# RetNet attention into a SwiGLU block in fp32: the gate/value products of the 1024-token tiles by Strassen's scheme applied twice, in place of a 26-product scheme

## The chip, the cores and the metric

One core of a Trainium2 chip runs the kernel. The metric is device microseconds of one execution; the runs of the kernel before took 1037.82, 1038.73 and 1038.70 us (median 1038.7). Engines are named as in the profile: PE (TensorE's matmuls), PEld (its weight loads), DVE (VectorE), ACT (ScalarE), POOL (GpSimd), SP (SyncE, which here issues DMAs).

## The reference

All arrays are fp32. Eight batches of eight heads, 576 positions, head size 64; the attention's heads are laid side by side to give 4608 tokens of 512 features, which go through a SwiGLU block with 1536 hidden features.

```python
scores = scale * np.matmul(q, k.transpose(0, 1, 3, 2))
Dmat = np.where(rel >= 0, gamma[:, None, None] ** rel[None, :, :], 0.0)
attn = np.matmul(scores * Dmat[None], v)
x = attn.transpose(0, 2, 1, 3).reshape(B * S, H * D)      # 4608 x 512
g, val = x @ w_gate, x @ w_val                            # 512 x 1536 each
return (g * (1.0 / (1.0 + np.exp(-g))) * val) @ w_out     # 1536 x 512
```

## The kernel before

The tokens are cut into a first tile of 512 (number 0, done with plain matmuls) and four tiles of 1024 (numbers 1 to 4). The attention of one batch and one pair of heads is a "tick"; it makes `x` for its tokens, and ticks for the next tile are spread through the current one, so tile 4 has none. Small pieces of a tick (copies, masks, decays, transposes) wait in the list `pieces` and are run by `part_on` between matmul steps; the last piece of a tick issues the loads of a later one (`next_load`) on SP.

Each 1024-token tile has an "up" stage (gate and value, `up_step`) and a "down" stage (`down_step`, output product). In the up stage, the 1536 hidden features are three "quarters" of 512 (`NQ` = 3, index `qd`; the name comes from the arena's layout). For a quarter, a 512x512 weight matrix (gate and value side by side) times 512x1024 of `x` is done by a scheme of 26 products. Its table `UP` gives for each of the 26 steps the bank, the sums of `x` and of weights to be made, the operands, and what to do with the result. A step is four matmuls of 128x128 by 256 columns (gate and value, two contraction halves) into one PSUM bank of 128x512. TensorE runs an fp32 matmul as two records, so a step shows as eight. Four banks (A, B, C, E) are used in rotation (`rested`).

What comes off a bank is copied by ACT, or added to an earlier partial result by DVE; `reads` also sends additions between partial results in SBUF to POOL (DVE in tile 1, partly). When a block of the hidden matrix is done, ACT applies Silu to its gate half into `io`, and DVE or POOL multiplies with the value half into `hid`.

Tile 1 differs: its weight sums are made then (`w_sums` on POOL, negations on ACT), and every weight operand is written to DRAM (`up_ops`, a DMA issued by ACT at line 1128). In tiles 2 to 4 the operands come back through a ring of eight SBUF slots (`fetch`, on SP, line 1022). The down stage's operands (`dn_ops`) come through the same ring; it overlaps the place of the weights, so that the first eight fetches of tile 1's down operands are made when weights are dead: at steps 21, 22 and 25 of the last quarter.

The order on every engine is the order in which the program is written (`manual_schedule`); `merge` interleaves ticks and steps evenly. Every queue runs in order, so a waiting instruction holds all behind it. SBUF is full: places are reused by hand (`part` for partial results, `xsum` for sums of `x`).

Of the kernel before, what the change touches and what calls it, by code (L numbers as in the profile page):

```python
# [22 lines left out]
def tables(gamma, scale, L):  # L23
# [27 lines left out]
UP = [  # L51
    "0= | 8: sub 8 2 6, sub 9 0 8, sub 10 4 9 | 8: neg 8 6, sub 9 2 6, sub 10 3 7, add 11 1 10 | copy 0, copy 1",
    "1= | 10: sub 11 3 8, sub 12 7 11 | 3: nad 12 3 6 | copy 2, copy 3",
    "2= | 0:  | 9:  | copy 4, copy 5",
    "3= | 12:  | 11: sub 8 11 6 | copy 6",
    "0+ | 9:  | 12: add 9 2 3 | sub 2 b 2, sub 4 4 2, out 4 4",
    "1= | 4: sub 13 0 2 | 10: nad 11 11 0 | add 2 b 2, neg 12 2",
    "3+ | 11: add 14 4 12 | 8:  | add 1 b 1",
    "0+ | 13: sub 15 14 0 | 9: add 12 4 5, add 10 2 12, nad 8 7 10 | sub 5 5 b, out 6 5",
    "1+ | 14: sub 16 0 1, add 17 5 16 | 11:  | add 6 b 6",  # L60
    "3= | 15: sub 18 4 6, sub 19 5 18 | 0: add 6 6 7 | add 7 b 6, neg 0 7",
    "2+ | 17:  | 8: sub 9 3 0 | copy 4",
    "0= | 19: add 20 7 10 | 5: add 11 0 2 | copy 5",
    "1= | 6:  | 6: add 7 7 5 | sub 0 b 0, out 14 0",
    "3+ | 20: sub 21 4 17 | 9: add 8 5 6 | sub 3 b 3",
    "2= | 3: sub 22 16 6 | 11: add 0 0 1 | add 7 b 3, out 7 7",
    "0+ | 21: add 18 18 7 | 7: nad 9 1 3 | add 2 b 2, sub 4 4 2, add 5 5 4",
    "1+ | 22:  | 8: sub 11 1 10 | add 2 b 2, neg 13 2",
    "3= | 18: sub 23 1 3, sub 24 5 23 | 0: nad 6 6 12 | add 6 b 6",
    "0= | 7:  | 9: add 2 2 4 | add 1 b 1, add 3 b 3, neg 15 1, neg 3 3, add 6 6 3, neg 2 6",  # L70
    "2+ | 24: sub 1 1 5 | 11: sub 12 0 12 | add 3 b 3",
    "1+ | 16:  | 6:  | sub 4 b 4",
    "3= | 1: sub 2 16 2 | 2: sub 1 5 1 | sub 5 b 5, add 0 b 4, out 8 5, out 9 0",
    "2+ | 23: sub 25 7 24 | 12: nad 3 3 10 | add 7 b 4, out 1 7",
    "1+ | 2:  | 4:  | neg 10 b",
    "3+ | 25:  | 1:  | sub 3 b 3, out 11 3",
    "0= | 5:  | 3:  | add 4 b 4, neg 5 4",
]
# [77 lines left out]
def kernel(  # L156
# [32 lines left out]
    nc = tc.nc  # L189
# [60 lines left out]
    at = [4096 + 512 * i for i in range(4)] + [x0_at + 512 * i for i in range(4)]  # L250
    at += [dn_at + 4096 + 512 * i for i in range(6)] + [part_at + 512 * i for i in range(4)]
    xsum = [rest[:, a : a + 512] for a in at]
    part = [rest[:, dn_at + 512 * i : dn_at + 512 * (i + 1)] for i in range(8)] + xsum[14:18]
# [642 lines left out]

    up, down = lines(UP), lines(DOWN)
    N = len(up)
# [13 lines left out]
    up_ops = [[dr.tile([P, 512], F32, name=f"up{qd}_{i}") for i in range(N)] for qd in range(NQ)]  # L912
# [85 lines left out]
    def up_view(qd):  # L998
        return lambda s: (w_up[:, qd, :, s // 2, s % 2, :] if s < 8
                          else extra[:, s - 8].rearrange("p (g x) -> p g x", g=2))  # L1000

    def x_view(n):
        return lambda s: (xs[n][:, 2 * (s // 4) : 2 * (s // 4) + 2, (s % 4) * TB : (s % 4 + 1) * TB] if s < 8
                          else xsum[s - 8].rearrange("p (c x) -> p c x", c=2))
# [6 lines left out]
    fetches = [("dn", 1, i) for i in range(N)]  # L1011
    for n in range(2, NTILE):
        fetches += [("up", qd, i) for qd in range(NQ) for i in range(N)] + [("dn", n, i) for i in range(N)]
    fetched = [0]
    turn = [5, 4, 1, 6, 7, 2, 0, 3]

    def fetch():
        m = fetched[0]
        if m < len(fetches):
            what, a, i = fetches[m]  # L1020
            src = up_ops[a][i] if what == "up" else dn_ops[i]
            nc.sync.dma_start(out=ring[:, turn[m % 8], 0 : src.shape[-1]], in_=src)
            fetched[0] += 1
# [22 lines left out]
    products = []  # L1046

    def reads(ops, bank, busy, result, spread=False):

        at = lambda a: bank if a == "b" else part[int(a)]  # L1050
        old = len(products)
        for op in ops:
            if op[0] in ("copy", "add", "sub"):
                while any(a == op[1] for a, _ in products):
                    products.pop(0)[1]()
                    old -= 1
            if op[0] == "copy":
                nc.scalar.copy(out=at(op[1]), in_=bank)
            elif op[0] in ("add", "sub"):
                eng = nc.vector if "b" in op or (busy and not spread) else nc.gpsimd  # L1060
                eng.tensor_tensor(out=at(op[1]), in0=at(op[2]), in1=at(op[3]),  # L1061
                                  op=ALU.add if op[0] == "add" else ALU.subtract)
            else:
                product = result(int(op[1]), at(op[2]), op[0] == "neg", op[2] == "b" or busy)
                if product and op[2] == "b":
                    product()
                elif product:
                    products.append((op[2], product))
        for _ in range(old):
            products.pop(0)[1]()  # L1070


    x_ops = [op for line in up for op in line[3]]
    X_FIRST = 8

    def x_sums(n, lo, hi, vector):
        for op in x_ops[lo:hi]:
            add(nc.vector if vector or op[0] == "nad" else nc.gpsimd, op, x_view(n))

    def negated(qd, i):  # L1080

        view = up_view(qd)
        for op in up[i][5]:
            if op[0] == "nad":
                nc.scalar.mul(out=view(int(op[1])), in_=view(int(op[3] if op[3] == op[1] else op[2])), mul=-1.0)

    def w_sums(qd, i):
        view = up_view(qd)
        for op in up[i][5]:
            if op[0] == "nad":  # L1090

                dst, a, b = [view(int(s)) for s in op[1:]]
                if op[3] == op[1]:
                    a, b = b, a
                nc.gpsimd.tensor_tensor(out=dst, in0=dst, in1=b, op=ALU.subtract)
            else:
                add(nc.gpsimd, op, view)

    def first_sums(qd, lo, hi):

        engines = [nc.scalar, nc.gpsimd, nc.vector, nc.gpsimd]
        for op, eng in list(zip(up[0][5], engines, strict=True))[lo:hi]:
            if op[0] == "neg":
                nc.scalar.mul(out=up_view(qd)(int(op[1])), in_=up_view(qd)(int(op[2])), mul=-1.0)
            else:
                add(eng, op, up_view(qd))

    def up_step(n, qd, i):
        label, opens, xslot, _, wslot, _, ops = up[i]
        busy = n == 1  # L1110
        if qd == 0:
            done = lambda i: X_FIRST + (min(3 * i, 2 * i + 2, i + 6) if busy else i)
            x_sums(n, done(i), done(i + 1), busy)
        if busy:
            if i > 1:
                w_sums(qd, i)
            w = up_view(qd)(wslot)
        else:
            w = operand()[:, 0:512].rearrange("p (g x) -> p g x", g=2)
        rhs = x_view(n)(xslot)  # L1120
        b = bank(label, i == 0)
        for gv in range(2):
            for c in range(2):
                m = nc.tensor.matmul(b[:, gv * TB : (gv + 1) * TB], w[:, gv, ts(c, P)], rhs[:, c, :],  # L1124
                                     start=(opens and gv == 0 and c == 0), stop=(c == 1), skip_group_check=True)
        stepped.append(m)
        if busy:
            nc.scalar.dma_start(out=up_ops[qd][i].rearrange("p (g x) -> p g x", g=2), in_=w)
            if i in (20, 23) and qd + 1 < NQ:
                first_sums(qd + 1, *((0, 2) if i == 20 else (2, 4)))  # L1130
            if i == 24 and qd + 1 < NQ:
                negated(qd + 1, 1)
                w_sums(qd + 1, 1)
            if 0 < i < N - 1:
                negated(qd, i + 1)
            if qd + 1 == NQ:
                for _ in range({21: 3, 22: 2, N - 1: 3}.get(i, 0)):
                    fetch()
        else:
            fetch()  # L1140

        def result(o, src, negative, vector):
            s = io[:, (silus[0] % 4) * TB : (silus[0] % 4 + 1) * TB]
            silus[0] += 1
            nc.scalar.activation(out=s, in_=src[:, 0:TB], func=AF.Silu, scale=-1.0 if negative else 1.0)  # L1145
            dst = hid[:, qd, o // 4, o % 4]
            if negative:
# [8 lines left out]
        if qd + 1 == NQ and i + 1 == N:  # L1156
            while products:
                products.pop(0)[1]()
# [187 lines left out]
```

## Time and profile before

| | us |
|---|---|
| median of three runs (lowest, highest) | 1038.7 (1037.82, 1038.73) |
| profiled execution, first to last instruction | 1037.2 |
| up stage of tile 1, 2, 3, 4 | 146.7, 145.2, 139.6, 134.6 |
| down stage of tile 1, 2, 3, 4 | 79.7, 77.1, 69.3, 71.0 |
| before tile 1 | 174.0 |

The profile comes from one execution. For it only the span is given: 1037.2 us, 1.5 below the median of the timed runs, and all working below is made against that span. Busy times are sums over the span or over a stated stretch; a chain of waits follows the last instruction back through what released it; a group of instructions shows count, busy time, mean duration, and idle time before with what ended it. PE records are pipelined, and their durations overlap; the time of a matmul is read from the spacing of steps. The granted clock was 0.998 over the span.

### The profile page before, as it was taken

How to read it: one execution, taken by the hardware profiler on the slowest of the kernel's cores; microseconds unless marked ns; L12 is line 12 of the kernel's file. 1: busy time of each engine (PE TensorE's matmuls, PEld its weight loads, DVE VectorE, ACT ScalarE, POOL GpSimd, SP SyncE). 2: the span in 40 equal slices, each digit the busy share in tenths (PEclk: the TensorE clock that was granted, in tenths of full speed). 3: DMA queues.
4: the chain of work that ended last, by engine and by line, in shares of the span. 5: the costliest groups of instructions: out<-in, count | busy, mean ns of one | idle time of the engine just before them, and what ended most of it. 6: DMA issues, size and time to landing. Idle time of an engine off the chain costs nothing.

```text
span 1037.2 us, 21564 instructions
## 1 busy us (share of the span) xinstructions
PE 1023.1 (99%) x8440; PEld 846.0 (82%) x8440; DVE 633.2 (61%) x1070; ACT 299.6 (29%) x653; POOL 419.9 (40%) x369
## 2 busy tenths in 40 slices
PE   6999999999999999999999999999999999999998
PEld 5654555888888888888888888888888888888887
DVE  4488878676768667446458685435465644344644
ACT  3566433253544222222322103223211022231110
POOL 3401265867564236522134057222242583222425
PEclk9999999999999999999999999999999999999999
DMA  9999877777679887674686686555554465555653
GB/s 240 258 279 263 200 218 269 204 205 191 196 194 265 211 244 220 177 197 133 188 231 173 176 208 208 153 142 153 159 171 148 143 196 153 153 153 160 182 163 100
DMA packets 307244, 199.12 MB, mean 192 GB/s; under 512 B 215944, under 2 KB 251784, under 8 KB 307144
## 3 DMA queue, kind: packets, MB, share of 16 engines
q1 hardware_dynamic: 275720, 161.17, 58.2%
q10 hardware_dynamic: 30784, 36.18, 10.4%
q8 instruction: 67, 1.10, 0.5%
q0 software_dynamic: 640, 0.39, 0.2%
q14 instruction: 33, 0.27, 0.1%
HBM read 157.58 MB, written 40.11 MB: 191 GB/s over the span
## 4 chain that ended last, share of the span: by engine, by line
PE 93%; DMA 3%; DVE 1%; ACT 1%; issue 1%; SPq 1%; POOL 0%; DVEq 0%; ACTq 0%; POOLq 0%
PE bankC L1124 13%; PE bankE L1124 13%; PE bankB L1124 13%; PE bankA L1124 13%; PE bankB L1173 7%; PE bankC L1173 7%; PE bankE L1173 7%; PE bankA L1173 7%; PE outer L556 2%; PE bankA L877 2%; PE bankB L877 1%; PE bankE L877 1%; PE outer L583 1%; PE inner L597 1%; PE inner L567 1%; PE bankC L877 1%
## 5 line engine op out<-in xcount | busy, mean ns | idle before, releaser
L1061 POOL TENSOR_TENSOR rest<-rest 128x512 f32<-128x512 f32 x65 | 91.7, 1415 | 234.3 <-DVE rest L1061 212.8
L1145 ACT ACTIVATE io<-rest 128x256 f32<-128x256 f32 x180 | 75.0, 416 | 305.4 <-DVE rest L1061 262.4
L1124 PE MATMUL bankC<-rest,arena 128*128 128x256 f32 x544 | 129.0, 380 | 0.0
L1124 PE MATMUL bankA<-rest,arena 128*128 128x256 f32 x544 | 128.7, 379 | 0.0
L910 POOL TENSOR_TENSOR arena<-arena 128x512 f32<-128x512 f32 (+1 forms) x72 | 110.6, 1549 | 37.3 <-DMA up<-arena 26.5
L1124 PE MATMUL bankB<-rest,arena 128*128 128x256 f32 x512 | 121.2, 380 | 0.5 <-DMA arena<-up 0.5
L1124 PE MATMUL bankE<-rest,arena 128*128 128x256 f32 x512 | 121.4, 380 | 0.1
L1152 POOL TENSOR_TENSOR arena<-rest,io 128x256 f32<-128x256 f32 x72 | 51.9, 726 | 167.7 <-ACT io L1145 167.7
L1124 PEld LDWEIGHTS bankA<-rest,arena 128*128 128x128 f32 x544 | 103.2, 190 | 14.5 <-issue 0.5
L1124 PEld LDWEIGHTS bankC<-rest,arena 128*128 128x128 f32 x544 | 102.9, 190 | 14.4 <-POOL arena L910 0.3
L1124 PEld LDWEIGHTS bankB<-rest,arena 128*128 128x128 f32 x512 | 97.0, 190 | 14.0 <-issue 0.8
L1124 PEld LDWEIGHTS bankE<-rest,arena 128*128 128x128 f32 x512 | 97.0, 190 | 13.7 <-DVE rest L1061 0.5
L910 POOL TENSOR_TENSOR rest<-rest 128x256 f32<-128x256 f32 (+1 forms) x69 | 68.9, 1020 | 71.8 <-DMA dn<-rest 35.3
L1061 DVE TENSOR_TENSOR rest<-bankB,rest 128x512 f32<-128x512 f32 x72 | 48.9, 687 | 67.1 <-PE bankB L1124 52.5
L1061 DVE TENSOR_TENSOR rest<-bankC,rest 128x512 f32<-128x512 f32 x72 | 48.9, 687 | 65.5 <-PE bankC L1124 46.9
L1061 DVE TENSOR_TENSOR rest<-bankA,rest 128x512 f32<-128x512 f32 x72 | 48.9, 687 | 61.2 <-PE bankA L1124 45.1
L1061 DVE TENSOR_TENSOR rest<-bankE,rest 128x512 f32<-128x512 f32 x71 | 48.2, 687 | 60.5 <-PE bankE L1124 47.1
L1148 DVE SCALAR_TENSOR_TENSOR arena<-rest,io 128x256 f32<-128x256 f32 x84 | 56.7, 676 | 10.8 <-ACT io L1145 10.8
L1173 PE MATMUL bankC<-arena 128*128 128x256 f32 x252 | 58.3, 380 | 0.1
L1173 PE MATMUL bankB<-arena 128*128 128x256 f32 x252 | 58.2, 381 | 0.0
L1173 PE MATMUL bankA<-arena 128*128 128x256 f32 x252 | 57.9, 379 | 0.0
L1173 PE MATMUL bankE<-arena 128*128 128x256 f32 x252 | 57.9, 379 | 0.0
(204 smaller groups left out, 1626.1 us busy)
## 6 DMA issues: line engine op xcount, KB each, us to landing
arena<-up SPq DMA_DIRECT2D x234, 256.0 KB, 2.6
arena<-dn SPq DMA_DIRECT2D x104, 384.0 KB, 3.8
up<-arena ACTq DMA_DIRECT2D x78, 256.0 KB, 3.7
dn<-rest SPq DMA_DIRECT2D x78, 128.0 KB, 1.8
out_dram<-rest SPq DMA_DIRECT2D x31, 256.0 KB, 3.9
qk<-in_q_dram SPq DMA_DIRECT2D x108, 72.0 KB, 2.6
qk<-in_k_dram SPq DMA_DIRECT2D x108, 72.0 KB, 2.7
rest<-in_moe_w_out_dram ACTq DMA_DIRECT2D x6, 1024.0 KB
```

The lines of the kernel that those rows point to most:

```text
L556: m = nc.tensor.matmul(value(i, hl, c), s["v"][rows, at], ret[rows, c % 2 if whole(i) else hl, c // 2], start=start, stop=start, skip_grou ...
L567: nc.tensor.matmul(z[half[hl], r, c], s["kn"][chunk(i, hl, 2 * c + r)], s["v"][rows, at], start=True, stop=True, skip_group_check=True)
L583: nc.tensor.matmul(xr[half[hl]] if c + 1 == NC else value(i, hl, c), state[half[hl], c, :], s["qT"][half[hl], ts(c, L)], start=False, stop ...
L597: nc.tensor.matmul(sc[chunk(i, hl, 2 * c + r)[0], r if whole(i) else hl, c], kT[half[hl], at], qT[half[hl], at], start=True, stop=True, sk ...
L877: nc.tensor.matmul(bank, w, xs[0][:, c, :], start=(c == 0), stop=(c == HP - 1))
L910: eng.tensor_tensor(out=dst, in0=srcs[0], in1=srcs[1], op=ALU.add if op[0] == "add" else ALU.subtract)
L1061: eng.tensor_tensor(out=at(op[1]), in0=at(op[2]), in1=at(op[3]), op=ALU.add if op[0] == "add" else ALU.subtract)
L1124: m = nc.tensor.matmul(b[:, gv * TB : (gv + 1) * TB], w[:, gv, ts(c, P)], rhs[:, c, :], start=(opens and gv == 0 and c == 0), stop=(c == 1 ...
L1145: nc.scalar.activation(out=s, in_=src[:, 0:TB], func=AF.Silu, scale=-1.0 if negative else 1.0)
L1148: return lambda: nc.vector.scalar_tensor_tensor(out=dst, in0=src[:, TB : 2 * TB], scalar=-1.0, in1=s, op0=ALU.mult, op1=ALU.mult)
L1152: nc.gpsimd.tensor_tensor(out=dst, in0=src[:, TB : 2 * TB], in1=s, op=ALU.mult)
L1173: nc.tensor.matmul(b[:, m * TB : (m + 1) * TB], lhs[:, qd, ts(m, P)], w[:, qd], start=(opens and qd == 0 and m == 0), stop=(qd == NQ - 1), ...
```

## The change

The 26-product table goes. The quarter's product is now cut in 2x2 blocks and done by Strassen's seven products (Winograd's form, with eight sums before), and each of the seven again in 2x2 blocks by the same form: 49 products. An inner product is 128x128 by 256 columns, for gate and value: a step is two matmuls, and a tile has 3 x 49 = 147 steps. The seven outer products come in the order `OUTER`; below, "scheme i" is the inner seven-product form that makes outer product i, and p1 to p7 are its steps.

```python
LEFT = {1: "11", 2: "12", 3: "s4", 4: "22", 5: "s1", 6: "s2", 7: "s3"}
RIGHT = {1: "11", 2: "21", 3: "22", 4: "t4", 5: "t1", 6: "t2", 7: "t3"}
SUMS = {
    "s1": ("add", "21", "22"), "s2": ("sub", "s1", "11"), "s3": ("sub", "11", "21"), "s4": ("sub", "12", "s2"),
    "t1": ("sub", "12", "11"), "t2": ("sub", "22", "t1"), "t3": ("sub", "22", "12"), "t4": ("sub", "21", "t2"),
}
OUTER = (1, 2, 6, 7, 4, 5, 3)
...
    seq = [(0, 1), (0, 5)]
    for m in range(MS):
        seq += [(m, p) for p in (6, 2, 3, 7)] + [(m + 1, p) for p in (1, 5) if m + 1 < MS] + [(m, 4)]
```

A scheme holds three of the four banks: x takes p1 and p2; z takes p5 and p3; y starts as ACT's copy of p1 (bank to bank) and takes p6, p7 and p4. What is read in between, and by whom, is in the new `exits` (`side` is DVE in tile 1 and POOL later; `from_` names an earlier partial result that is added):

```python
        if p == 1:
            r["y"] = rested.pop(0)
            nc.scalar.copy(out=wide(r["y"]), in_=b)
            return
        if p in (5, 6):
            ...
            if from_ is None:
                nc.scalar.copy(out=at, in_=b)
            elif n == 1:
                src = source(name)
                nc.vector.tensor_tensor(out=at, in0=b, in1=src, op=ALU.add)
            else:
                nc.scalar.copy(out=at, in_=b)
                src = source(name)
                nc.gpsimd.tensor_tensor(out=at, in0=at, in1=src, op=ALU.add)
            ...
            return
        name, row, col = SPOT[p]
        if p in (3, 7):
            at = r.pop(name)
            nc.vector.tensor_tensor(out=at, in0=b, in1=at, op=ALU.add)
        elif from_ is None and i == 1:
            at = take(hold(i))
            nc.scalar.copy(out=at, in_=b)
        elif from_ is not None:
            ...
            nc.vector.tensor_tensor(out=at, in0=b, in1=src, op=ALU.add)
        else:
            at = b
        ...
        wait = 2
        if i == 5:
            t, v = values.pop((qd, "t", name)), values.pop((qd, "v", name))
            eng = nc.vector if p in (2, 4) else side
            eng.tensor_tensor(out=t, in0=at, in1=t, op=ALU.add)
            eng.tensor_tensor(out=v, in0=at, in1=v, op=ALU.add)
            values[qd, "n", name] = t
            if p in (3, 7):
                room.append(at)
                wait = 4
            at = v
        r_, c_ = FINAL[i]
        finish(n, at, qd, 2 * (1 - r_) + row, 2 * (1 - c_) + col, wait)
```

`finish` places the Silu on ACT `wait` steps later, and the product one step after it, on DVE in tile 1 and on POOL later:

```python
            nc.scalar.activation(out=s, in_=at[:, 0], func=AF.Silu)
            behind(1, lambda: product(s))
        ...
            (nc.vector if n == 1 else nc.gpsimd).tensor_tensor(out=hid[:, qd, f, t], in0=at[:, 1], in1=s, op=ALU.mult)
```

The sums of `x` (32 a tile: four of 128x1024 elements and 28 of 128x256; the first eight before the stage) are all on DVE, placed six steps ahead and one step apart. The sums of weights in tile 1 (132 of 128x256) are all on POOL, five steps ahead and 0.9 steps apart, each written to a free place or over a block that has had its last use; no weight is negated any more. Every step of tile 1 writes its operand to DRAM by a DMA of 128 KB issued by ACT (147, before 78 of 256 KB). Tiles 2 to 4 fetch two steps' operands by one DMA of 256 KB. The first eight fetches of tile 1's down operands come after the last step of its up stage, into ring slots in the order in which they died:

```diff
         merge((0.0, ticks(done, cut)), (0.5, ups))
         if n == 1:
+            turn[:] = ring_order()
+            for _ in range(8):
+                fetch()
```

A piece of a tick is run after p1, p5 and p4 (three times in seven steps of half the length), before after nearly every step. The down stage keeps its 26 products; its additions without a bank operand are still POOL's.

## Prediction

> **What bounds the kernel now.** I read the page first: its first line, the busy shares and the chain that ended last.
>
> ```profile
> span 1037.2 us, 21564 instructions
> PE 1023.1 (99%) x8440; PEld 846.0 (82%) x8440; DVE 633.2 (61%) x1070; ACT 299.6 (29%) x653; POOL 419.9 (40%) x369
> ...
> PE 93%; DMA 3%; DVE 1%; ACT 1%; issue 1%; SPq 1%; POOL 0%; DVEq 0%; ACTq 0%; POOLq 0%
> ```
>
> TensorE is the bound: busy 99%, 93% of the chain. Next, the waits of TensorE alone: its matmuls of the gate/value stage (L1124) appear once.
>
> ```profile
> PE bankB L1124 <- DMA arena<-up: 0.5, 1, 0.5
> ```
>
> So everything around L1124 is hidden today. Then busy time by stage, the eight stretches being up and down of tiles 1 to 4 (boundaries read from the chain; columns: stretch, length, busy us and count of PE, PEld, DVE, ACT, POOL, clock, DMA share, GB/s).
>
> ```profile
> 174.00:320.70 146.70, 146.58 (x1238) 127.95 (x1237) 105.12 (x176) 62.58 (x138) 96.58 (x73) 1.00 0.74 209
> 400.40:545.60 145.20, 144.74 (x1170) 126.91 (x1169) 76.13 (x144) 39.31 (x87) 49.73 (x50) 1.00 0.67 188
> 622.70:762.30 139.60, 139.60 (x899) 122.78 (x897) 67.99 (x117) 36.97 (x81) 51.35 (x51) 1.00 0.58 167
> 831.60:966.20 134.60, 134.60 (x625) 118.51 (x624) 56.73 (x88) 34.41 (x74) 49.59 (x49) 1.00 0.59 165
> ```
>
> The tile 4 stage has no attention work: 134.6 us for 78 steps of four matmuls is 1.726 us a step, 0.4315 us a matmul. The other stages are longer by their attention ticks: 12.1, 10.6 and 5.0 us. In tile 1 DVE is already busy 105 of 147 us. Last, the groups by form (busy us and mean ns behind the bar):
>
> ```profile
> L1061 POOL TENSOR_TENSOR rest<-rest 128x512 f32<-128x512 f32 x65 | 91.7, 1415 | 234.3 <-DVE rest L1061 212.8 <-issue 17.6 <-PE bankE L1124 2.6
> L1152 POOL TENSOR_TENSOR arena<-rest,io 128x256 f32<-128x256 f32 x72 | 51.9, 726 | 167.7 <-ACT io L1145 167.7
> L1061 DVE TENSOR_TENSOR rest<-bankC,rest 128x512 f32<-128x512 f32 x72 | 48.9, 687 | 65.5 <-PE bankC L1124 46.9 <-PE bankC L1173 10.8 <-POOL rest L1061 7.4
> L910 POOL TENSOR_TENSOR rest<-rest 128x256 f32<-128x256 f32 x43 | 34.1, 817 | 71.3 <-DMA dn<-rest 35.3 <-DVE rest L431 35.2
> L1058 ACT COPY rest<-bankA 128x512 f32<-128x512 f32 x36 | 20.2, 590 | 49.4 <-PE bankA L1173 36.3 <-PE bankA L1124 11.3 <-DMA out_dram<-rest 1.8
> ```
>
> and the single lines' spreads (min/median/max ns):
>
> ```profile
> L1148 DVE SCALAR_TENSOR_TENSOR arena<-rest,io x84: 381/425/1953, 189.5 to 967.5; 128x256 f32<-128x256 f32 x84
> L910 DVE TENSOR_TENSOR rest<-x_odd,rest x16: 674/692/1759, 165.6 to 621.4; 128x512 f32<-128x512 f32 x16
> L1061 POOL TENSOR_TENSOR rest<-rest x65: 1260/1275/1912, 202.8 to 1031.1; 128x512 f32<-128x512 f32 x65
> ```
>
> A DVE op with both operands in SBUF is short when alone (0.42 us for 256 elements, 0.69 for 512) but up to 1.95 beside POOL; one that reads a bank stays at 0.69 (0.64 to 0.69). In tile 1 the 46 SBUF products (L1148, L1151) took 33.4 us there, 0.725 each.
>
> **TensorE's share.** 49 products of two matmuls replace 26 of four: 98 for 104 a quarter, 18 fewer a tile (three quarters), 72 in all. 72 x 0.4315 = 31.1 us less, 7.8 a tile. A step is now 0.863 us (147 a tile), half of before, and this is what the rest must fit. A bank is needed again two steps after its last matmul (p3 to the next scheme's p5, p6 to p7, p7 to p4): 1.73 us. A 0.69 read that starts some 0.26 us after the step (timeline: matmuls of a step follow 1.73 us apart, DVE starts 0.26 into the next) leaves 0.8 us to spare. Before, the queues behind a bank were waited for by nothing.
>
> **Tile 1: DVE.** The weight sums go to POOL (132 x 0.82 = 108 us, less than the stage). DVE gets every exit addition, product and x sum:
> - 128x512 adds: per quarter 5 schemes x 6, 2 in scheme 1, 10 in scheme 5, 42; three quarters 126, of which 114 read a bank: 114 x 0.687 = 78.3; the other 12 between 0.69 and 1.76;
> - 48 products and 24 x sums of 256 elements, between 0.42 and the 1.95 of the row;
> - attention ticks: 12 transposes x 0.76 and five sets of 2.9 us: 23.7.
> Which value beside POOL? The extra of the row, 0.725 - 0.42 = 0.31, came beside POOL adds of about 1.34 us (L910, 512 elements); the new ones are 0.82, so 0.31 x 0.82/1.34 = 0.19: 0.61 a product, 0.88 for 512. Sum: 78.3 + 12 x 0.88 + 72 x 0.61 + 23.7 = 156.5 us. At the undisturbed ends it is 140.5, at the row's own 0.725 (512: 1.02) 166.4. TensorE needs 126.9 + 12.1 = 139.0. Moreover the load is lumpy and TensorE can run ahead by two steps only. In order, by groups of seven steps (6.04 us of TensorE), DVE needs 8.4, 7.2, 6.6, 7.9 and 11.8 in the first quarter from the third group on, 7.9 and 13.3 (against 8.4 with a tick) at the end of the second, 7.9 and 12.7 at the end of the third. The heavy group is scheme 5's tail: 11 adds and 6 short ops, 11 x 0.69 + 6 x 0.61 + 0.4. The excess, 2.4+1.2+0.6+1.9+5.8+1.9+4.9+1.9+6.7 = 27 us, goes on top of 139: 166. With undisturbed ops the same sum by groups is 153, with the row's 173. I take 165: **+18 us** against 146.7 (+6 to +26).
>
> A rule bears on this. The Trainium skill, SBUF — State Buffer, Who interferes with whom, says that a DVE instruction with two SBUF inputs and a GpSimd instruction that reads SBUF exclude each other for a whole instruction. By that rule, an arrival would wait half of 0.82 us in the two thirds of the time that POOL is busy, 0.27 instead of 0.19, and the group sum would be 170, an estimate 5 us above mine.
>
> **Tiles 2 to 4: POOL.** Here scheme 5's p3 and p7 send four 128x512 adds to POOL, at 1.275 undisturbed, and the p5 and p6 additions of the following scheme 3 queue behind them. Count from the end of p3 (scheme 5). DVE's two adds of p2 and its p3 exit are done at 1.5; POOL's four adds end at 2.8, 4.1, 5.4, 6.65. ACT's Silu of p7 stands ahead of its copy of scheme 3's p6, and waits for the fourth: copy done at 6.65 + 0.45 + 0.65 = 7.75. p7 of scheme 3 writes that bank and would start at 6.04: **1.75 us lost**. POOL goes on: product 7.4, p5 add 8.65, product 9.4, p6 add 10.65; DVE's p7 exit 11.4; p4 wanted that bank at 10.4: 1.05 lost. So 2.8 us in quarters one and two. In the last quarter no next scheme stands between p7 and p4: p4 would start at 6.9 and starts at 11.4, 4.5 lost. A tile: 2.8 + 2.8 + 4.5 = 10.1, three tiles 30.3. POOL beside x sums (1.9) would add up to 2 us a quarter; if ACT or the sums came earlier than I order them, nothing remains: 0 to 45. The x sums lift DVE to 6.9 and 7.0 in two groups of tiles 2 and 3, +1.8 each: 3.6.
>
> **The smaller parts.** ACT's copy from bank to bank (84) has no row; bounds are 0.37 (256 elements from a bank) and 0.69, and I take the 0.59 of a 512 copy to SBUF: with 1.73 us for it, it hides while ACT isn't held. ACT issues 147 write-outs for 78 (0.32 to 0.78 us each, beside its running instruction); they delay its next instruction by at most that, inside DVE's slack: 0, or up to 0.3 x 147 = 44 if ACT loses its cover. The tile 1 fetches of down operands, before at steps 21, 22 and 25 of the last quarter, now stand on SP after the whole stage, and after the last tick's ten loads, which wait for its key transpose some 7 us before the end: ten issues of 0.35, then 3.8 to landing, less two: first operand 0 to 7 us late, +3 taken. It delays the out stage's first step alone. 219 fetches for 234, same bytes a us: nothing.
>
> **Sum.** Against the profiled span of 1037.2: tile 1 +18, tiles 2 to 4 -23.3 + 30.3 + 3.6 = +10.6, fetch +3: 1069 us. The median of the runs lies 1.5 above that span: **1070 us**.
>
> **Rivals.**
> (1) TensorE stays the bound. For it: 99% busy, no wait in L1124, POOL 34 to 37% and ACT 26% busy in tiles 2 to 4; the burst is only seen in my ordering. Price: -31.1, thus 1008; with 3 to 20 us of small stalls, 1011 to 1028. It decides if all new waits together stay below 31 us, which needs DVE's tile 1 load to run near 140 us and POOL's four adds to be absorbed. DVE's group sum even undisturbed (153) speaks against it. Chance 0.20.
> (2) The tile 1 load is real, the burst isn't: 1038.7 + 18 - 23.3 + 3.6 + 3 = 1040, 1028 to 1048. Chance 0.12.
> (3) Weights come late as well: POOL's sums overwrite slots whose write-out just started (step 109's slot is rewritten for step 112, 2.6 us later, while a write-out took 3.7 to land), and the doubled issues hold ACT: another 20 to 40 us in tile 1, 1090 to 1110. Against it: DVE's pace stretches that stage anyway. Chance 0.10.
> The forecast, DVE in tile 1 and POOL's burst later, 1048 to 1090: 0.58.
>
> **Numbers.** A difference of 0.2% (2 us) is about what a measurement tells from none. Slower: 0.58 + 0.10 + 0.07 of (2) = 0.75; same 0.02; faster 0.20 + 0.03 = 0.23. The range leaves out half of (1) and most of (3): 1018 to 1095; the forecast's own is 1048 to 1090.
>
> **What would show it.** Right: matmul count down by 72 (twice that in records); DVE over 90% busy in the tile 1 stage, which lasts over 155 us; PE waits on ACT and DVE at scheme 3's p7 and p4, about 1.8 and 4.5 us, in tiles 2 to 4, with POOL's four adds before; stages of 137 to 150 us there. Wrong: stages at 139, 137, 132 and 127 us with no waits (rival 1); waits of PE for POOL or write-outs in tile 1 (rival 3); a mean of the 256-element DVE ops far from 0.61.

## The result, and the profile after

The changed kernel took 1085.7 us (median of four runs, 1084.3 to 1087.3), the kernel before 1038.7 (1037.8 to 1038.8) on the same chip: a ratio of 1.045, 95% interval 1.044 to 1.047. The forecast was 1070, range 1018 to 1095. The profiled span is 1084.3 us, 47.1 above the 1037.2 of before.

The page first: its first line, the busy shares, the granted clock in 40 slices, and the chain that ended last.

```profile
span 1084.3 us, 22116 instructions
...
PE 1014.2 (94%) x8296; PEld 822.0 (76%) x8296; DVE 699.7 (65%) x1201; ACT 360.0 (33%) x770; POOL 537.5 (50%) x549
...
PEclk9999999989997999999998999999989999999999
...
PE 76%; DVE 9%; POOL 8%; DMA 4%; issue 2%; ACT 1%; SPq 0%; ACTq 0%; DVEq 0%; POOLq 0%
```

TensorE has 144 records fewer (72 matmuls of two records), as counted. But it is busy 94% for 99%, and DVE and POOL hold 17% of the chain for 1%. New too: four dips in the clock. Before, the records show no half clock (a granted clock of 0.5) between 21.9 us and the last 2 us; now they show it for 37.5 us before the last 2 us, in periods of 3.41, 6.83 and 10.24.

TensorE's waits (line, who is waited for: us in total, times, longest; L1251 is the matmul of `up_step`, L1292 and L1303 are DVE's exits of p5/p6 and of p3/p7, L1294 is ACT's copy of p5/p6):

```profile
PE bankC L1251 <- DVE rest L1303: 7.1, 4, 3.1
PE bankB L1251 <- DVE rest L1303: 6.5, 3, 3.1
PE bankA L1343 <- DMA arena<-dn: 5.8, 1, 5.8
...
PE bankC L1251 <- DVE rest L1292: 3.1, 3, 1.9
PE bankA L1251 <- ACT rest L1294: 2.6, 2, 1.5
```

Where before one wait of 0.5 us stood, TensorE now idles 18.0 us in tile 1, 17.2 of it for DVE's exits; then 5.8 for the first down operand; and 10.1, 11.3 and 10.1 us in tiles 2 to 4.

The four up stages (length; busy us and count of PE, PEld, DVE, ACT, POOL; clock; DMA share; GB/s). The first includes the 5.8 us of the fetch:

```profile
173.40:345.96 172.56, 148.69 (x1201) 121.99 (x1199) 143.26 (x251) 58.10 (x133) 102.77 (x128) 0.95 0.72 182
...
427.10:578.50 151.40, 141.17 (x1136) 121.13 (x1133) 90.16 (x167) 61.56 (x129) 88.61 (x91) 0.98 0.63 174
...
655.60:803.70 148.10, 136.68 (x867) 116.95 (x861) 82.32 (x143) 59.20 (x123) 89.66 (x92) 0.98 0.50 151
...
872.80:1011.75 138.95, 128.84 (x590) 111.22 (x589) 69.13 (x111) 56.49 (x116) 86.57 (x89) 1.00 0.52 157
```

| up stage, us | tile 1 (without the fetch) | tile 2 | tile 3 | tile 4 |
|---|---|---|---|---|
| before | 146.7 | 145.2 | 139.6 | 134.6 |
| forecast | 165 | 149.3 | 143.7 | 136.9 |
| after | 166.8 | 151.4 | 148.1 | 139.0 |

That is 20.1 + 6.2 + 8.5 + 4.4 = 39.2 us; the fetch adds 5.8, and the down stages of tiles 1 and 4 are 1.4 and 1.5 longer, each beginning with about 3 us at half clock; that of tile 3 and the stretch before tile 1 are 0.2 and 0.6 shorter.

The burst of the forecast can be read in the timeline of tile 4, first quarter (start, length, engine, line, tile; in brackets idle time before, and its releaser). L1322 and L1323 are scheme 5's t and v additions, L1296 the p5/p6 addition of scheme 3, all on POOL:

```profile
912.72 1.45 POOL L1323 TENSOR_TENSOR arena<-arena 128x512 f32<-128x512 f32 x1
...
914.20 0.42 ACT L1178 ACTIVATE io<-arena 128x256 f32<-128x256 f32 x1 [2.23 <-POOL arena L1323]
914.52 0.57 ACT L1294 COPY rest<-bankA 128x512 f32<-128x512 f32 x1
914.81 1.26 POOL L1296 TENSOR_TENSOR rest<-rest 128x512 f32<-128x512 f32 x1
...
915.14 1.13 PE L1251 MATMUL bankA<-rest,arena 128*128 128x256 f32 x4 [1.53 <-ACT rest L1294]
...
918.01 0.69 DVE L1303 TENSOR_TENSOR rest<-bankB,rest 128x512 f32<-128x512 f32 x1 [4.37 <-POOL rest L1296]
918.62 0.68 DVE L1303 TENSOR_TENSOR rest<-bankA,rest 128x512 f32<-128x512 f32 x1
...
918.76 0.70 PE L1251 MATMUL bankB<-rest,arena 128*128 128x256 f32 x2 [1.62 <-DVE rest L1303]
...
919.73 1.03 PE L1251 MATMUL bankA<-rest,arena 128*128 128x256 f32 x4
```

Silu waits 2.23 us for the fourth addition; the copy that would free bank A stands behind it in ACT's queue; p7 starts 1.53 us late. Then DVE's exit of p3 waits for POOL's p6 addition, and p5 of the next quarter's first scheme, which takes bank B from p3, starts 1.62 late; p7's exit ends at 919.30, before p4 (bank A, the last line) is due, so p4 has no wait of its own. At the end of a tile no next scheme stands between, and there it is p4 that waits, 3.08 us in each of tiles 2 to 4.

### The profile page after: what moved, and what is told of

Its sections match the earlier page's. It is cut to its first block, busy times and chain, and to the rows that moved or that the text cites. A ratio compares the mean times of both kernels' runs of the same rounds, so it can differ in the third digit from the quotient of the medians.

```text
span 1084.3 us, 22116 instructions
## 1 busy us (share of the span) xinstructions
PE 1014.2 (94%) x8296; PEld 822.0 (76%) x8296; DVE 699.7 (65%) x1201; ACT 360.0 (33%) x770; POOL 537.5 (50%) x549
## 4 chain that ended last, share of the span: by engine, by line
PE 76%; DVE 9%; POOL 8%; DMA 4%; issue 2%; ACT 1%; SPq 0%; ACTq 0%; DVEq 0%; POOLq 0%
PE bankB L1251 9%; PE bankE L1251 9%; PE bankA L1251 9%; PE bankC L1251 8%; PE bankA L1343 6%; PE bankE L1343 6%; PE bankB L1343 6%; PE bankC L1343 6%; PE outer L538 2%; POOL rest L1322 2%; POOL rest L1296 2%; DVE rest L1303 2%; PE bankA L859 2%; PE bankB L859 2%; PE inner L579 1%
## 5 line engine op out<-in xcount | busy, mean ns | idle before, releaser
L1251 PE MATMUL bankC<-rest,arena 128*128 128x256 f32 x492 | 129.2, 386 | 10.1 <-DVE rest L1303 7.1
L1251 PE MATMUL bankA<-rest,arena 128*128 128x256 f32 x492 | 129.5, 386 | 9.5 <-DVE rest L1303 4.7
L1251 PE MATMUL bankB<-rest,arena 128*128 128x256 f32 x492 | 128.3, 383 | 9.4 <-DVE rest L1303 6.5
L1251 PE MATMUL bankE<-rest,arena 128*128 128x256 f32 x492 | 127.9, 383 | 8.5 <-DVE rest L1303 4.3
L1069 POOL TENSOR_TENSOR arena<-arena 128x256 f32<-128x256 f32 x132 | 104.7, 810 | 52.9 <-DMA up<-arena 37.1
L1251 PEld LDWEIGHTS bankA<-rest,arena 128*128 128x128 f32 x492 | 93.2, 192 | 26.7 <-DVE rest L1303 7.1
L1251 PEld LDWEIGHTS bankC<-rest,arena 128*128 128x128 f32 x492 | 93.5, 192 | 26.0 <-POOL arena L1069 3.7
L1251 PEld LDWEIGHTS bankB<-rest,arena 128*128 128x128 f32 x492 | 93.2, 191 | 25.1 <-DVE rest L1303 7.7
L1251 PEld LDWEIGHTS bankE<-rest,arena 128*128 128x128 f32 x492 | 93.0, 191 | 24.4 <-DVE rest L1303 6.4
L1178 ACT ACTIVATE io<-rest 128x256 f32<-128x256 f32 x135 | 55.9, 416 | 124.1 <-DVE rest L1310 50.6
L1296 POOL TENSOR_TENSOR rest<-rest 128x512 f32<-128x512 f32 x51 | 65.3, 1281 | 45.3 <-ACT rest L1294 27.4
L1182 POOL TENSOR_TENSOR arena<-rest,io 128x256 f32<-128x256 f32 x87 | 64.2, 748 | 35.7 <-ACT io L1178 35.2
L892 POOL TENSOR_TENSOR rest<-rest 128x256 f32<-128x256 f32 x43 | 34.7, 829 | 71.1 <-DVE rest L413 37.1
L1069 DVE TENSOR_TENSOR rest<-rest 128x256 f32<-128x256 f32 (+1 forms) x88 | 61.5, 721 | 0.2
L1343 PEld LDWEIGHTS bankA<-arena 128*128 128x128 f32 x252 | 48.8, 194 | 13.4 <-DMA arena<-dn 6.5
L1343 PEld LDWEIGHTS bankE<-arena 128*128 128x128 f32 x252 | 48.9, 195 | 7.1
L590 ACT COPY even<-inner 128x256 f32<-128x256 f32 x32 | 11.9, 371 | 126.4 <-PE inner L579 107.6
```

The source lines that it names most:

```text
L892: eng.tensor_tensor(out=dst, in0=srcs[0], in1=srcs[1], op=ALU.add if op[0] == "add" else ALU.subtract)
L1069: eng.tensor_tensor(out=out, in0=a, in1=b, op=ALU.add if kind == "add" else ALU.subtract)
L1178: nc.scalar.activation(out=s, in_=at[:, 0], func=AF.Silu)
L1182: (nc.vector if n == 1 else nc.gpsimd).tensor_tensor(out=hid[:, qd, f, t], in0=at[:, 1], in1=s, op=ALU.mult)
L1251: mm = nc.tensor.matmul(b[:, gv * TB : (gv + 1) * TB], w[:, gv], rhs, start=(opens and gv == 0), stop=True, skip_group_check=True)
L1296: nc.gpsimd.tensor_tensor(out=at, in0=at, in1=src, op=ALU.add)
```

## The experiments

The question was whether the 47 us are DVE's and POOL's load, or the order in their queues, and what the clock adds. Ratios are to the kernel before on the same chip; its medians lay between 1038.7 and 1042.2.

### One suspect at a time

**POOL's burst moved to DVE.**

```diff
-        side = nc.vector if n == 1 else nc.gpsimd
+        side = nc.vector
```

> Scheme 5's additions behind p3 and p7 are made by DVE in every tile (they were POOL's in tiles 2 to 4). Theory (POOL's four additions hold ACT's Silu and the p5 and p6 additions of scheme 3, and the half clock follows those stalls): the pairs of PE waits at the end of each quarter of tiles 2 to 4 go; the up stages fall from 151.4, 148.1 and 139.0 us to about 139, 133 and 128, the time to 1046 to 1050 us. Rival (the banks' two steps are too short for any engine; DVE gets late in POOL's place): waits of the same size move to DVE, 1075 to 1085 us. Rival (the half clock has nothing to do with stalls): the half-clock periods at the ends of tiles 2, 3 and 4 stay.

Measured 1072.7 us, ratio 1.030 (1.027 to 1.033), just below the rival's range and far above the theory's. The up stages of tiles 2 to 4 took 148.3, 140.5 and 133.1, 16.6 less than after; the idle time there is 8.9, 6.2 and 4.8 us, 19.9 for 31.5. The burst is real, but much of its price stayed: the same additions now stand ahead of DVE's exits. Scheme 5's p4 waits 1.0 to 1.1 us for those in every quarter, the tile's last p4 1.1, and the first p1 or p5 of the second quarter 0.6 to 1.7. No half-clock period is left in tiles 2 to 4, whose longest stall is now 1.7 us; three of 6.8 us remain in tile 1 and at its end. So the half clock goes with the longer stalls.

**The Silu behind the burst, later.**

```diff
-                wait = 4
+                wait = 4 if n == 1 else 7
```

> In tiles 2 to 4 the Silu of scheme 5's p3 and p7 results is placed seven steps later, not four, so that it stands behind ACT's copy of scheme 3's p6. Theory: the first wait of each pair (PE on ACT, 1.1 to 1.5 us, nine times) goes, but POOL's p5 and p6 additions still come after its four additions, so that most of it comes back as a wait on DVE's exits: 0.8 us less a quarter, 5 to 9 us in all, 1076 to 1081 us. Rival (ACT's place in the queue was the cause): both waits go, 25 us or more less, below 1062 us.

Measured 1088.0 us, ratio 1.044 (1.041 to 1.048), as the changed kernel; the 5 to 9 us of the theory did not come. ACT's copy is free, and each quarter's pair of waits became one, of 2.7, 2.4 and 3.8 us in tile 4; idle is 8.9, 9.7 and 8.9 us a tile, 4 us less in all. Taking away the first wait of a chain mostly made the second longer, and two of the single waits of 2.7 us brought half-clock periods of 3.41 us that the pairs had not.

**Half of tile 1's products to POOL** (those of schemes 5 and 3).

```diff
-    def finish(n, at, qd, f, t, wait):
+    def finish(n, at, qd, f, t, wait, pool=True):
...
-            (nc.vector if n == 1 else nc.gpsimd).tensor_tensor(out=hid[:, qd, f, t], in0=at[:, 1], in1=s, op=ALU.mult)
+            (nc.gpsimd if pool else nc.vector).tensor_tensor(out=hid[:, qd, f, t], in0=at[:, 1], in1=s, op=ALU.mult)
...
-        finish(n, at, qd, 2 * (1 - r_) + row, 2 * (1 - c_) + col, wait)
+        finish(n, at, qd, 2 * (1 - r_) + row, 2 * (1 - c_) + col, wait, n > 1 or i in (5, 3))
```

> In tile 1 the products of schemes 5 and 3 (24 of 48) are made by POOL, not by DVE. Theory (DVE's lumps bound tile 1): DVE has 15 us less, all in the heavy groups at the end of each quarter; the tile 1 stage falls from 172.6 us by 10 to 18, the time to 1067 to 1076 us, and half-clock periods in tile 1 get fewer. Rival (POOL bounds tile 1 through late weight sums and the write-outs that they wait for): no gain or a loss, 1083 to 1092 us, with PE waits on POOL.

Measured 1081.8 us, ratio 1.039 (1.034 to 1.044), outside both ranges. Tile 1's stage fell by 7.5 us, the fetch included, less than the 10 expected, and TensorE still idles 12.9 us in it.

**All of tile 1's products to POOL.**

```diff
-            (nc.vector if n == 1 else nc.gpsimd).tensor_tensor(out=hid[:, qd, f, t], in0=at[:, 1], in1=s, op=ALU.mult)
+            nc.gpsimd.tensor_tensor(out=hid[:, qd, f, t], in0=at[:, 1], in1=s, op=ALU.mult)
```

> All 48 products of tile 1 on POOL, 30 us less for DVE and 35 more for POOL. Theory (DVE bounds tile 1): the tile 1 stage falls to 152 to 160 us (after: 172.6; 24 products on POOL: 165.1). Rival (by then POOL's weight sums come late): 163 us or more, with PE waits on POOL's weight sums.

Measured 1083.7 us (two runs), ratio 1.041 (1.037 to 1.044). DVE's busy time in tile 1 fell to 119.4 us, yet the stage without its fetch wait took 156.9, for 158.9 with half the products moved. With that wait, as the expectation counts it, it is 162.6, above the theory's 160; of the rival's waits for POOL there are 2.1 us. DVE's load alone is not what bounds this stage.

**The fetches of tile 1's down operands, early.**

```diff
+            for _ in range({137: 2, 139: 1}.get(s, 0)):
+                fetch()
...
+            turn[:] = [6, 7, 5, 3, 0, 2, 1, 4]
...
-            turn[:] = ring_order()
-            for _ in range(8):
+            for _ in range(5):
```

> Three of the first eight fetches of tile 1's down operands are issued after steps 137 and 139, ahead of the last tick's loads on SP, into the three ring slots that are dead by then. Theory (the fetch stands behind ten tick loads): the 5.8 us wait of PE for the first down operand goes, 4 to 6 us less, 1080 to 1082 us. Rival (the DMA engines are the limit there): the wait stays within 2 us of 5.8.

Measured 1081.8 us, ratio 1.039 (1.036 to 1.042). The 5.8 us wait is gone, and nothing took its place.

**Stalls put into the kernel before.** In tile 4, step 13 of each quarter, DVE copies the step's `x` operand onto itself 1, 4 and 9 times, so that TensorE waits for DVE once a quarter in an otherwise full stage.

```diff
+        for _ in range({(0, 13): 1, (1, 13): 4, (2, 13): 9}.get((qd, i), 0) if n == 4 else 0):
+            nc.vector.tensor_copy(out=rhs, in_=rhs)
```

> The kernel before, with three waits put into tile 4's up stage (step 13 of each quarter): DVE copies that step's x operand onto itself 1, 4 and 9 times, and TensorE waits for it. Theory (an idle time of TensorE of some us halves the granted clock for a multiple of 3.4 us): no half-clock period after the first wait of about 1.3 us, one or two periods after the last of about 5, the second in between; the time is longer than before by the waits (about 9 us) and half of the periods. Rival (the half clock comes with the changed kernel's denser weight loads or operands): clock 1.00 throughout tile 4.

One run, 1055.0 us. TensorE's waits (L1126 is the matmul of the kernel before, L1122 the copy):

```profile
PE bankB L1126 <- DVE rest L1122: 5.2, 1, 5.2
...
PE bankE L1126 <- DVE rest L1122: 2.9, 1, 2.9
...
PE bankC L1126 <- DVE rest L1122: 1.1, 1, 1.1
```

After the stall of 1.12 us the granted clock stayed full; with the one of 2.90 us came 3.41 us at half clock, with the one of 5.21 us 6.83. The stage grew from 134.6 to 148.2 us for 9.2 us of idle time. Of the 4.4 us above it, half of the 7.2 us in which TensorE worked at half clock makes 3.6, and 0.8 is left, about 0.25 a stall.

The length of a stall does not decide alone: a stall of 2.24 us in the run with exits first brought half clock, and one of 2.84 in the last kernel did not (both below). The clock's records show what does. In every trace of this case the clock changes only at points that lie whole multiples of 3.413 us apart. Cut at these points (from 170 us to 8 us before the end), the fourteen traces have 3543 windows at full clock. Of the 40 in which TensorE was idle for more than 1.93 us, all were followed by half clock; of the 3482 with less than 1.70, none; of the 21 between, 9. The stall of 2.24 us lay within one window; the one of 2.84 was split between two, with 1.72 in the larger part.

### Together, and the order in the queues

**Three edits at once**: DVE additions, half the products on POOL, early fetch (the edits shown above).

> The three edits together: scheme 5's additions behind p3 and p7 on DVE in every tile, the products of schemes 5 and 3 of tile 1 on POOL, three early fetches of down operands. Theory (three separate losses, each followed by its own half-clock periods): the gains add, 16 + 7 + 6 us by the single runs' ratios, so 1055 to 1060 us against 1039 to 1042 before, still slower than before. Rival (they share a cause, so that one removes what another did): less than 20 us below the changed kernel, above 1065 us.

Measured 1055.2 us, ratio 1.013 (1.010 to 1.016). The gains add, as the theory had it. Up stages 156.8, 149.4, 139.7, 133.2; idle 12.6, 8.0, 5.5, 4.8 us.

**The t additions back to POOL, the v additions of p3 and p7 two steps later on DVE** (three in tile 1), with the other two edits.

```diff
-            eng.tensor_tensor(out=v, in0=at, in1=v, op=ALU.add)
+            def add_v(out=v, a=at, done=p in (3, 7)):
+                nc.vector.tensor_tensor(out=out, in0=a, in1=out, op=ALU.add)
+                if done:
+                    room.append(a)
...
+                behind(3 if n == 1 else 2, add_v)
...
+            else:
+                add_v()
```

> As the run of the three edits, but scheme 5's lump is spread: behind p3 and p7 one of the two additions stays at once (POOL in tiles 2 to 4, DVE in tile 1), the other is made by DVE two steps later (three in tile 1). Theory (a wait comes from additions queued ahead of the next exit, not from the engines' totals): the remaining waits of 1.0 to 1.7 us at the ends of quarters shrink to 0.5 or less, tiles 2 to 4 fall to about 142, 135 and 129 us, the time to 1035 to 1048 us. Rival (DVE's and POOL's totals matter, or they hold each other on SBUF): as the three edits within 5 us.

A miss: 1056.3 us, ratio 1.014 (1.008 to 1.019), where the rival had it. POOL's additions and its p5/p6 work hold scheme 3's exits again, with waits of 0.6 to 2.7 us and 20.1 us of idle time in tiles 2 to 4, for 18.4. So spreading alone gains nothing. Whether load or what stands ahead of an exit decides, this run does not tell; the next ones do.

**Exits first.** From the three edits: p3's two additions go out two steps later, behind p7's exit; the v additions of p3 and p7 go to POOL; the p6 addition is one DVE instruction from the bank.

```diff
-            elif n == 1:
+            elif n == 1 or p == 6:
...
+            eng = nc.vector if p in (2, 4) else nc.gpsimd
+
+            def sums(part=at):
+                nc.vector.tensor_tensor(out=t, in0=part, in1=t, op=ALU.add)
+                eng.tensor_tensor(out=v, in0=part, in1=v, op=ALU.add)
+                if p in (3, 7):
+                    room.append(part)
+
+            if p == 3:
+                behind(2, sums)
+            else:
+                sums()
```

> From the kernel of the three edits (additions on VectorE, last products of tile 1 on GpSimd, early fetch; 1055, up stages 156.8, 149.4, 139.7, 133.2 us) with three more changes: scheme 5's p3 sends its two SBUF additions two steps later, so that p7's exit stands ahead of them on VectorE; the v addition of p3 and p7 goes to GpSimd in all tiles; and the p6 addition of tiles 2 to 4 is one VectorE instruction straight from the bank, so that no Silu stands ahead of a copy that frees a bank. Theory (TensorE waits because a bank's exit stands behind additions that nobody waits for): the quarter's wait of 1.06 us goes, the tile's last wait of about 1.1 us stays since p4 follows p7 at once there; idle in tiles 2 to 4 falls from 8.0, 5.5 and 4.8 to 2 to 4 us each, tile 1 loses 2 to 6 us; 1036 to 1048 us in all. Rival (VectorE's load itself is the limit, the order is not): waits only change place, 1052 to 1060 us.

Measured 1051.0 us, ratio 1.010 (1.007 to 1.012), between the two ranges. Idle time in tiles 2 to 4 fell to 6.9, 4.5 and 3.1 us; in tile 1 it stayed at 12.6. Most of what is left in tile 4, 2.24 us, stands in one place, in the first quarter (timeline; L1325 is the t addition, L1326 the v addition, L1069 an x sum):

```profile
884.99 1.71 POOL L1326 TENSOR_TENSOR arena<-arena 128x512 f32<-128x512 f32 x1 [1.80 <-DVE arena L1304]
885.49 1.75 DVE L1325 TENSOR_TENSOR rest<-rest 128x512 f32<-128x512 f32 x1
...
886.66 1.71 POOL L1326 TENSOR_TENSOR arena<-rest,arena 128x512 f32<-128x512 f32 x1
887.17 1.48 DVE L1069 TENSOR_TENSOR rest<-rest 128x256 f32<-128x256 f32 x1
...
889.77 0.97 DVE L1069 TENSOR_TENSOR rest<-rest 128x256 f32<-128x256 f32 x1
...
891.40 1.35 PE L1251 MATMUL bankA<-rest,arena 128*128 128x256 f32 x4 [2.24 <-DVE rest L1293]
```

A 128x512 addition from SBUF takes 1.75 us on DVE and 1.71 on POOL here, 0.69 and 1.27 undisturbed; a 256-element x sum takes 1.48 for 0.42. These x sums are needed much later, but stand ahead of p6's exit. In tile 1, 8.5 of the 12.6 us are for weight sums (the next expectation gives 7.1 of 10.3, too little by the trace): POOL waited for p3's exits, 18.5 us in all, with the weight sums behind in its queue.

**x sums ahead of the tail**; in tile 1 the v additions back on DVE.

```diff
-        x_times[:] = spaced([e[0] for e in x_ops[n][X_FIRST:]], 6, 1.0)
+        x_times[:] = spaced([min(e[0], 43) for e in x_ops[n][X_FIRST:]], 6, 1.0)
...
-            eng = nc.vector if p in (2, 4) else nc.gpsimd
+            eng = nc.vector if p in (2, 4) or n == 1 else nc.gpsimd
```

> The kernel that puts exits first (1051; its up stages 157.6, 147.8, 138.2, 132.7 us) with the last x sums of each tile issued before step 38, ahead of scheme 5's tail in the first quarter, where two of them took 1.48 and 0.97 us beside GpSimd and left a bank 2.2 us late (5.0 in tile 2); and with the v additions of tile 1 back on VectorE, since on GpSimd they waited for their input for 5 to 7 us with weight sums queued behind (7.1 of the 10.3 us that TensorE idled in tile 1). Theory (order, not load): tiles 2 to 4 lose 2 to 5 us each (145, 136, 130.5), tile 1 stays within 3 us of 157; 1040 to 1046. Rival (VectorE's load): the waits come back at other steps, tiles 2 to 4 within 1 us of before, 1050 to 1055.

Measured 1044.2 us, ratio 1.002 (1.000 to 1.005). Tiles 2 to 4 took 145.1, 136.8 and 128.7, idle 4.5, 3.2 and 0.9: the same instructions, earlier in the queue, and the stages 8.0 us shorter in all. DVE's busy time there fell by 3.7 us, mostly because the x sums are shorter away from POOL's additions (11.8 us in tile 4, 12.9 before); how much of the gain is this and how much the order alone, no run separates. Tile 1 took 160.5, a little more than expected.

**Weight sums nine steps ahead**, and tile 1's v additions on POOL.

```diff
-    X_FIRST, W_LEAD, W_GAP = 8, 5, 0.9
+    X_FIRST, W_LEAD, W_GAP = 8, 9, 0.9
```

> As the kernel with the early x sums, but tile 1's v additions stay on GpSimd and the weight sums are issued 9 steps ahead of their use in place of 5, so that they stand before those additions in GpSimd's queue. Theory: the 7.1 us of waits for weight sums in tile 1 go, the stage takes 150 to 153 us; 1034 to 1041 in all, which is level with or faster than the kernel before (1039). Rival (sums wait for the write-outs of the slots they overwrite, so an earlier place does not help): tile 1 stays at 155 to 158, 1041 to 1047.

Measured 1038.3 us, ratio 0.997 (0.995 to 1.000), level with the kernel before. TensorE idles 9.7, 4.6, 2.4 and 0.9 us in tiles 1 to 4 (the next expectation gives less for tiles 1 and 3). Tile 1 took 152.8; POOL still waits there for p3's exits, but most weight sums are already made: TensorE's waits for them fell from 8.5 to 1.7 us. POOL's waits in tile 1:

```profile
POOL arena L1069 <- DMA up<-arena: 14.2, 16, 3.3
POOL rest L1326 <- DVE rest L1304: 13.0, 3, 6.4
```

**p4's additions two steps later, and the products of tile 1's first quarter on POOL.**

```diff
-            if p == 3:
+            if p in (3, 4):
...
-... wait, n > 1 or i in (5, 3))
+... wait, n > 1 or qd == 0 or i in (5, 3))
```

> The version with the longer lead (1038; up stages 152.8, 144.8, 136.1, 128.7 us; TensorE idle 7.4, 4.5, 1.5, 0.9) with two more changes: scheme 5's p4 sends its two additions two steps later, so that scheme 3's p6 exit stands ahead of them (the 2.75 us wait in tile 2, behind an attention step, and 1.35 in tile 1), and the products of tile 1's first quarter, where VectorE is busy 42.5 of 48.9 us and GpSimd 36.6, go to GpSimd. Theory (order, and in tile 1 VectorE's load): tile 2 loses 2 to 4 us with its half-clock period, tile 1 loses 1 to 4; 1031 to 1036, faster than the kernel before by 0.3 to 0.8%. Rival (what is left is load that no order removes): 1037 to 1040.

Measured 1033.6 us (six runs, 1031.5 to 1035.7), ratio 0.993 (0.990 to 0.995): faster than both kernels, by 0.7% than the one before. The page:

```profile
span 1033.9 us, 22010 instructions
...
PEclk9999999999999999999999999999999999999999
```

Its up stages of tiles 1 and 4 (columns as above):

```profile
179.03:328.96 149.93, 142.21 (x1201) 119.83 (x1200) 119.10 (x209) 57.60 (x132) 122.38 (x159) 1.00 0.78 202
...
833.80:962.48 128.68, 127.33 (x590) 111.38 (x588) 83.81 (x132) 48.57 (x101) 61.66 (x67) 1.00 0.59 169
```

No half-clock period is left between 16.5 us and the last 0.3. Tile 4 is 5.9 us below before, near the 7.8 that fewer matmuls are worth; one wait of 1.35 us (1.80 in tile 1) stays at each tile's end, where p4 needs the bank that p7 has just left. DVE is busy 84 us in tile 4 for 69 after the change (POOL 62 for 87), so more work on DVE in the right order is faster than less in the wrong one. Tile 1 is 3.2 above before.

## Why the prediction was right, and where it was off

- **TensorE's share.** 72 matmuls less, 7.8 us a tile: shown, most plainly by the last kernel's tile 4 (5.9 us less, with one wait of 1.35 left).
- **Tile 1's size was hit (166.8 for 165), its reason in part.** The durations of DVE's instructions in the stage add up to 154.3 us, forecast 156.5; the products' mean is 0.60, forecast 0.61, and that of 128x512 additions from SBUF 0.87, forecast 0.88. By the prediction's estimate from the skill's rule of exclusion (the Trainium skill, SBUF — State Buffer, Who interferes with whom), a 256-element operation would have taken about 0.69; the x sums did (0.69), the products did not. A pair side by side fits the rule: in the run with exits first, additions from SBUF took 1.75 us on DVE and 1.71 on POOL, not far from the 1.96 of both one after the other. But busy time is 139.8 of 166.8 us, 84% and not over 90: additions in a row follow each other after 0.60 us (median of 97) though each record lasts 0.68, and the forecast summed records. And the hit is partly luck. The forecast put 27 us of waits for DVE on top of 139; TensorE idled 18.0. The other 9.9 us are half clock (10.3 us in which TensorE worked at it, worth 5.2) and 4.7 more, about 0.25 for each of 18 stalls; the forecast had a term for neither. The limit is not the load alone. With DVE busy 119 us the stage took 156.9 us in one order (all products on POOL) and 149.9 in another (the last kernel), with POOL busy 126 and 122. The groups of seven steps named the right place, scheme 5's tail; but the forecast took DVE's load for the limit where the order in its queue counts as well.
- **POOL's burst.** 10.1 us a tile forecast; idle 10.1, 11.3 and 10.1 measured, of which 1.2 in tile 3 is another wait (p3 of scheme 1, for a copy of ACT). This mechanism was right nearly to the instruction: in tile 4's first quarter POOL's four additions end 2.7, 4.1, 5.4 and 6.8 us after p3, forecast 2.8 to 6.65. One step was misread: p3's exit, which also needs POOL's p6 addition, stands ahead of p7's in DVE's queue, so that in the first two quarters the second wait is that of the next scheme's p5, not of p4. It costs 1.62 for 1.05 there, the first 1.53 for 1.75; at the tile's end they are 1.1 and 3.08 for 4.5. The 3.6 for x sums on top did not show as such; the idle total, 31.5, is below the 33.9 of both terms.
- **The fetch.** +3 forecast from 0 to 7, 5.8 measured: this term was too small.
- **What the sum lacked.** Tiles 2 to 4 lost 19.1 us, forecast 10.6, though they idled no longer than forecast. Against the ideal stages (before less 7.8) they lost 14.0, 16.3 and 12.2, 11.0 more than their idle time. The records show 14.1 us at half clock at the ends of these stages; in 10.2 of them TensorE worked, which is worth 5.1. The rest, 5.9, over 19 stalls, is 0.3 a stall, near the 0.25 of the inserted waits; what it consists of is not shown. The forecast priced a stall at its own length; it had no term for the clock after it. The kernel before, at full clock from 21.9 us to its last 2, could not show one. The Trainium skill (TensorE: Matmul & The Clock Gate, Part 1: The HAM clock gate) states that the array falls back to half clock after an idle window of some 3.4 us and returns after a busy one. The periods of 3.41 us here fit that length, but the rule read as a threshold would have foreseen no half clock, since no stall of tiles 2 to 4 lasts over 3.1 us: an inserted stall of 2.90 was enough. By the records here, a little over half of such a window idle is enough.
- **The difference of 15.5 us** between 31.6 forecast and 47.1 measured: tiles 2 to 4 8.5, the fetch 2.8, tile 1 2.1, two down stages that begin at half clock 2.9; the 0.8 us of shorter stretches go off it.
- **The rivals.** TensorE did not stay the bound (1), and the burst is real (2). Late weights (3) fall for the changed kernel: TensorE waited 0.3 us for POOL's sums, though POOL itself waited 37.1 us for write-outs. They came up in the run with exits first (8.5 us), when additions that wait were put before them in POOL's queue. ACT's bank-to-bank copy, taken as 0.59, took 0.57.
- **Open.** What the 0.25 to 0.3 us a stall above its own length are is not shown. Nor was it tried what keeps tile 1 of the last kernel above 146.7: 7.6 us of idle time are left there, 2.8 of them for a p1 copy of ACT.

## What to carry to other kernels

When steps get shorter, list for each bank or buffer what its release stands behind in the queue of the engine that releases it; additions that nobody waits for go behind the release, even if the engine then does more in all. Removing the first wait of such a chain gives little until the second is gone as well. And price stalls of TensorE at more than their length: here 0.25 to 0.3 us more for each, and half of a half-clock period of 3.41 us or more wherever over about 1.9 us of idle time fell into one window of 3.413.

## What was not expected of the hardware

- In a stage in which TensorE is otherwise full, a single stall of 1.12 us left the granted clock alone, one of 2.90 us brought 3.41 us at half clock and one of 5.21 us 6.83. In all traces it went with the idle time within one window of a grid of 3.413 us, with the turn between 1.70 and 1.93 us, so that a stall of 2.24 us can bring half clock and one of 2.84 need not. In the changed kernel, two stalls of 1.1 and 3.1 us some 4 us apart brought 3.41 or 6.83 us; pairs of 1.5 and 1.6 in tile 4 none.
- DVE additions of 128x512 from a bank, back to back, start every 0.60 us, while each record lasts 0.68.
